# Transposing q and k by DMA from the ninth pair on, with both kinds of scores in one PE visit

## The chip, the cores and the metric

One core of one Trainium2 chip. The time is the device time of a whole execution in microseconds. Ratios are computed as the mean time of one kernel's fast runs over that of the other's fast runs in the same rounds, so they are not quite the ratio of the medians quoted beside them. An interval is the 95% interval of that ratio. "Slow" marks a run more than 1.5% above the fastest of the same kernel; such runs are left out of ratios.

## The reference, cut to what matters

Two attentions over 8 x 8 heads of 576 tokens and 64 dimensions are added, and the sum goes through an MLP.

```python
def _attn_ref(q, k, v):
    # q_d, k_d, v_d: means of groups of 4 tokens (144 groups)
    out_d = sm_attn(q_d, k_d, v_d)              # full attention over the groups
    out_up = np.repeat(out_d, 4, axis=2)
    mask = np.abs(pos[:, None] - pos[None, :]) < 4
    scores = np.where(mask, 0.125 * q @ k.T, -1e9)  # local attention, a band of 7
    ...
    return out_up + softmax(scores) @ v

def _moe_ref(x, w_in, w_out):                   # 4608 x 512 -> 2048 -> 512
    h = x @ w_in
    return (h / (1 + np.exp(-h))) @ w_out
```

## The kernel before

Heads go in 32 pairs. The Python program has a planner: it simulates the engines with a guessed cost for each instruction, takes whatever it believes ready, and so fixes at build time the order of instructions on each engine and on each DMA queue. On the chip every engine and queue works strictly in that order, waiting on semaphores. Pairs 0 to 7 ("direct") use another form of the softmax sums and of the v means; the change leaves them alone.

For a pair from the ninth on, the parts that matter:

```python
def load_qk(p):      # SP queue: qs, ks, 96 partitions x (2 heads x 6 tokens x 64), float32
def cast(p):         # POOL: qs -> qb, ks -> kb, bf16
def ph_T(p):         # PE: 6 + 6 transposes of 96 x 128 into PSUM
    ...
        P.op("PE", lambda t: t.transpose(tps[:, 96*c:96*c+96], w, id_bf[:, :]), ...)
    # out of PSUM, tokens put in their order on the way
    P.op("DVE", lambda e: e.tensor_copy(dst[0], src[0]), ...)          # qT
    P.op("ACT", lambda e: e.activation(dst[1], src[1], AF.Copy), ...)  # kT
def do_mean(p, nm):  # DVE: sums of 4 tokens, qT -> qd, kT -> kd
def ph_S1(p):        # PE: 8 local scores (row mode), ACT: exp
def ph_S2(p):        # PE: 2 local + 4 group scores, ACT: exp
def ph_Z(z):         # PE: softmax sums of two pairs; ACT: zc
    for o in range(4):                       # four copies of one partition to ten
        P.op("SP", dma_start(zr[10*o:10*o+10, :], zsrc[32*o:32*o+1, :] ...), ...)
def do_recip(z):     # DVE: rr = 1/zr; SP: scr (device memory) <- rr
def do_bcast(z):     # SP: four broadcasts Rb <- scr
def ph_PV(p):        # PE: attention x v;  DVE: xo = that x Rb;  POOL: xT += xo
```

"Row mode" is a setting of PE in which a matmul uses 64 of its 128 rows. The attention works through two PSUM buffers called duo. The MLP's first matmul (hps) reads xT; its second (ops) gives the output. In the planner every DMA of the SP queue is charged 450 units of issue and lands 2200 units after its bytes:

```python
t += 450 if eng == "SP" else 650 if eng == "ACT" else 800
...
q[0][0].end = t + 2200
```

The softmax here doesn't subtract the row's maximum and nothing guards it: scores larger than these inputs give would overflow.

## Time and profile before

| | before |
|---|---|
| median (range) of the 3 runs known at the prediction | 410.2 us (408.15 to 411.78) |
| span of the profiled run, granted clock (share of full speed that PE was given) | 410.4 us, 0.978 |
| PE busy over the span | 363.9 us (89%) |
| SP queue issuing in the stage of pairs 8 to 31 | 78% |

The lines that carry the reading are in the prediction. One row more, since the pace of the stage is read from it: the groups of q summed on DVE, once in each pair from 8 to 31 (minimum/median/maximum ns, first and last start in us).

```profile
L407 DVE TENSOR_REDUCE qd<-qT x24: 685/744/754, 86.2 to 284.8; 128x144 bf16<-128x576 bf16 x24
```

From 86.2 to 284.8 us there are 23 periods of 8.63 us. "SP issuing" is worked out from the timeline of the SP queue: the union of its issue intervals between these two starts, over their distance. The timeline shows successive issues of one line as one row with the gaps between them; without these gaps the figures of this kind are 0.1 to 0.4 us per pair lower. Issuing of a DMA doesn't count as busy in the profile's own tables, so such a queue has no row of its own in the page.

### The profile page before, as it was taken

Reading aid. Unit: us, or ns where it says so; the run is one execution under the profiler, and the core shown is the slowest. Engines: PE = TensorE matmul, PEld = TensorE weight load, DVE = VectorE, ACT = ScalarE, POOL = GpSimd, SP = SyncE. Lnnn points to the kernel's source line nnn. Section 1 sums busy time; section 2 is a strip of 40 time slices with the busy share of each in tenths; the row PEclk is TensorE's granted clock in tenths of the full one; section 3 lists DMA queues with packets and bytes.
Section 4 is the critical chain, followed back from the end, with each engine's and each line's share of the span. In section 5 each row is a group of like instructions: output and inputs, shape, how many; then the busy total and the mean of one; then the engine's idle time right before and its main releaser. Section 6 shows DMA issues by size and latency. Waiting matters only on the chain.

```text
span 410.4 us, 7839 instructions
## 1 busy us (share of the span) xinstructions
PE 363.9 (89%) x3145; PEld 232.8 (57%) x3184; DVE 229.5 (56%) x341; ACT 218.6 (53%) x378; POOL 181.8 (44%) x257
## 2 busy tenths in 40 slices
PE   1445889998899999979999798989999999999996
PEld 1225868676556556645656455655565555565552
DVE  1340342885667668787788877787645343343320
ACT  3361155854785567655776556757543444344331
POOL 7998456843943286376274627644404000000000
PEclk9999886999999999998999999999999999999999
DMA  6489743899899859886989954996232000101012
GB/s 172 98 194 316 196 91 89 177 212 204 190 214 245 238 134 235 172 220 176 245 225 207 194 184 136 253 187 168 98 102 88 26 26 33 46 27 51 26 53 77
DMA packets 77628, 61.81 MB, mean 151 GB/s; under 512 B 46616, under 2 KB 67864, under 8 KB 77592
## 3 DMA queue, kind: packets, MB, share of 16 engines
q1 hardware_dynamic: 73368, 55.02, 55.5%
q0 software_dynamic: 4224, 6.29, 6.9%
q8 instruction: 25, 0.41, 0.5%
q14 instruction: 11, 0.09, 0.1%
HBM read 53.67 MB, written 9.58 MB: 154 GB/s over the span
## 4 chain that ended last, share of the span: by engine, by line
PE 71%; POOL 8%; DMA 8%; ACT 4%; DVE 4%; issue 3%; SPq 1%; POOLq 0%; ACTq 0%
PE hps L378 29%; PE ops L378 28%; PE duo L378 11%; DMA vs<-in_v_dram 6%; PE duo L388 3%; DVE Pt L443 2%; DMA zr<-zc 2%; POOL hs L402 2%; ACT vb L354 1%; ACT th L640 1%; POOL qb L349 1%; POOL xo L512 1%; POOL kb L349 1%; POOL w_in_sb L668 1%; ACT Rb L577 1%
## 5 line engine op out<-in xcount | busy, mean ns | idle before, releaser
L378 PE MATMUL hps<-xT,w_in_sb 128*128 128x512 f32 x576 | 175.6, 431 | 0.8 <-DVE gT L642 0.7
L642 DVE SCALAR_TENSOR_TENSOR gT<-th,hps 128x512 bf16<-128x512 f32 x144 | 98.7, 687 | 108.0 <-ACT th L640 107.2
L378 PE MATMUL ops<-w_out_bf,gT 128*128 128x512 bf16 x537 | 139.0, 383 | 4.2 <-issue 2.9
L640 ACT ACTIVATE th<-hps 128x512 f32<-128x512 f32 x144 | 86.0, 597 | 94.4 <-PE hps L378 94.1
L378 PEld LDWEIGHTS hps<-xT,w_in_sb 128*128 128x128 f32 x576 | 106.0, 189 | 32.2 <-DVE gT L642 2.5
L378 PEld LDWEIGHTS ops<-w_out_bf,gT 128*128 128x128 bf16 x576 | 46.4, 98 | 65.0 <-issue 23.1
L617 POOL TENSOR_TENSOR xT<-xo 128x576 fp32r<-128x576 f32 (+2 forms) x40 | 40.7, 1031 | 92.7 <-DVE xo L600 92.4
L443 DVE TENSOR_TENSOR Pt<-Pt,mask_bf 128x1152 bf16<-128x1152 bf16 x32 | 38.0, 1188 | 19.5 <-ACT Pt L435 19.3
L349 POOL CAST qb<-qs 96x768 bf16<-96x768 f32 x31 | 27.1, 874 | 20.3 <-DMA qs<-in_q_dram 14.3
L359 POOL TENSOR_TENSOR vt<-vq 72x512 f32<-72x512 f32 x24 | 32.3, 1347 | 8.2 <-DMA vq<-in_v_dram 7.5
L661 ACT ACTIVATE osb<-ops 128x512 f32<-128x512 f32 x36 | 21.6, 599 | 21.6 <-PE ops L378 21.4
L420 ACT ACTIVATE Pt<-duo 128x912 bf16<-128x912 f32 x32 | 29.7, 927 | 3.6 <-PE duo L378 3.5
L354 ACT ACTIVATE vb<-vs 128x640 bf16<-128x640 f32 x32 | 23.4, 732 | 14.3 <-DMA vs<-in_v_dram 9.8
L598 DVE TENSOR_TENSOR xo<-duo,Rb 128x456 f32<-128x456 f32 x32 | 20.0, 624 | 19.4 <-PE duo L378 18.6
L393 DVE COPY qT<-duo 128x576 bf16<-128x576 bf16 x32 | 23.9, 750 | 10.7 <-PE duo L388 10.4
L349 POOL CAST kb<-ks 96x768 bf16<-96x768 f32 x31 | 25.7, 829 | 3.2 <-DMA ks<-in_k_dram 3.2
L378 PE MATMUL duo<-gT 128*128 128x90 f32 x128 | 23.5, 361 | 3.7 <-POOL gT L516 3.2
L378 PEld LDWEIGHTS duo<-gT 128*128 128x128 f32 x128 | 22.9, 274 | 4.4 <-POOL gT L516 3.5
L378 PE MATMUL duo<-qT,kT 64*128 64x112 bf16 (+1 forms) x320 | 20.4, 226 | 4.0 <-DVE xo L598 1.3
L394 ACT ACTIVATE kT<-duo 128x576 bf16<-128x576 bf16 x32 | 20.8, 649 | 4.2 <-PE duo L388 4.0
L388 PE MATMUL duo<-id_bf,qb 96*128 96x96 bf16 x192 | 14.6, 216 | 7.4 <-POOL xo L303 4.7
L378 PEld LDWEIGHTS duo<-qT,kT 64*128 64x128 bf16 x320 | 11.0, 99 | 17.6 <-issue 6.5
(65 smaller groups left out, 301.0 us busy)
## 6 DMA issues: line engine op xcount, KB each, us to landing
vs<-in_v_dram SPq DMA_DIRECT2D x64, 160.0 KB, 4.2
qs<-in_q_dram SPq DMA_DIRECT2D x32, 288.0 KB, 5.1
ks<-in_k_dram SPq DMA_DIRECT2D x32, 288.0 KB, 5.9
out_dram<-osb SPq DMA_DIRECT2D x36, 256.0 KB, 2.1
Rb<-scr SPq DMA_DIRECT2D x48, 180.0 KB, 3.8
vq<-in_v_dram SPq DMA_DIRECT2D x24, 256.0 KB
w_in_sb<-in_moe_w_in_dram POOLq DMA_DIRECT2D x4, 1024.0 KB, 8.1
w_out_bf<-in_moe_w_out_dram POOLq DMA_DIRECT2D x4, 512.0 KB, 14.5
```

What stands on the lines that cost most here:

```text
L349: pool(lambda g, d=dst, s=src: g.tensor_copy(d, s), r=[R(f"{nm}s{i}")], w=[R(f"{nm}b{j}")], cost=830)
L354: P.op("ACT", lambda e: e.activation(vb[m][:, :, :], vs[i][:, :, :], AF.Copy), r=[R(f"vs{i}")], w=[R(f"vb{m}")], cost=730)
L359: pool(lambda g: g.tensor_tensor(vt[:, :, :], vq[i][:, :, 0:128], vq[i][:, :, 128:256], ALU.add), r=[R(f"vq{i}")], w=[R("vt")], cost=1290)
L378: return P.op("PE", lambda t: t.matmul(out_, lhsT, rhs, start=start, stop=stop, skip_group_check=True), r, w, cost=cost)
L388: P.op("PE", lambda t, c=c, w=w, tps=tps: t.transpose(tps[:, 96 * c:96 * c + 96], w, id_bf[:, :]), r=[R("id"), R(f"{nm}b{j}")], w=[bk[x]], ...
L393: P.op("DVE", lambda e: e.tensor_copy(dst[0], src[0]), r=[bk[0]], w=[R(f"qT{j}")], cost=800)
L420: P.op("ACT", lambda e: e.activation(Pt[m][:, :, 0:456], D[:, :, 0:456], AF.Exp, scale=0.125), r=bk, w=[R(f"P{m}")], cost=930)
L443: P.op("DVE", lambda e: e.tensor_tensor(Pt[m][:, :, :], Pt[m][:, :, :], mask_bf[:, :].unsqueeze(1).to_broadcast([128, 2, S_]), ALU.mult), ...
L617: P.op("POOL", lambda e, dst=dst, in0=in0, in1=in1: e.tensor_tensor(dst, in0, in1, ALU.add), r=[R(f"xo{x}")], w=xblk(kc, t, e_), cost=200 ...
L640: P.op("ACT", lambda e: e.activation(th[tb][:, :], hps[hb][:, :], AF.Tanh, scale=0.5), r=[R(f"h{hb}", True)], w=[R(f"th{tb}")], cost=600)
L642: P.op("DVE", lambda e: e.scalar_tensor_tensor(gT[j % 2][:, f, :], th[tb][:, :], 1.0, hps[hb][:, :], ALU.add, ALU.mult), r=[R(f"h{hb}", Tr ...
L661: P.op("ACT", lambda e: e.activation(osb[s_][:, :], ops[ob][:, :], AF.Copy, scale=0.5), r=[R(f"o{ob}", True)], w=[R(f"osb{s_}")], cost=600)
```

## The change

Its intent is to take the transposes off PE, the fullest engine. The casts qb and kb are transposed between SBUF buffers by DMA; DVE and ACT then put the tokens in order from SBUF instead of from PSUM; and since both kinds of scores can now be formed at once, they share one visit of PE in row mode. The core of the diff:

```diff
+        qr = sb("qr", [128, 6, 96], BF16, 2)
+        kr = sb("kr", [128, 6, 96], BF16, 2)
...
+        def load_T(p, x):
+            j = p % 2
+            src, dst = (qb, qr) if x == "q" else (kb, kr)
+            P.op("SP", lambda e: e.dma_start_transpose(
+                dst[j][:, :, :], src[j][:, :, :, :].rearrange("p c h d -> p (c h d)")),
+                r=[R(f"{x}b{j}")], w=[R(f"{x}r{j}")], dma=f"{x}r{j}", cost=700)
+            P.free["SP"] += 700
+
+        def order_T(p, x):
+            j, y = p % 2, p % NQT
+            src = (qr if x == "q" else kr)[j][:, :, :].rearrange("p r g -> p g r")
+            dst = (qT if x == "q" else kT)[y][:, :].rearrange("p (g r) -> p g r", r=6)
+            if x == "q":
+                P.op("DVE", lambda e: e.tensor_copy(dst, src), ...)
+            else:
+                P.op("ACT", lambda e: e.activation(dst, src, AF.Copy), ...)
...
-            task(attn, f"T{p}", "PE", [f"c{p}", nm("S2", p - 2)], ...)
-            task(attn, f"S1{p}", "PE", [f"T{p}", nm("PV", p - NP_)], ...)
-            task(attn, f"S2{p}", "PE", [f"S1{p}", f"mq{p}", f"mk{p}"], ...)
+            if p in direct:
+                ...                                  # as before
+            else:
+                task(attn, f"S2{p}", "PE", [tq, tk, f"mq{p}", f"mk{p}", nm("PV", p - NP_)], ...,
+                     lambda: [R(f"duo{d}{x}", True) for d in range(2) for x in "ab"],
+                     lambda p=p: (ph_S1(p), ph_S2(p)), "row")
```

More of the change, by code (lines that the diff above doesn't have):

```diff
@@ L249, in bass_hourglass_attn__then__act_silu_kernel @@
         vd = sb("vd", [72, 4, 64], BF16, NVB)
-        qT = sb("qT", [128, S_], BF16, 2)
-        kT = sb("kT", [128, S_], BF16, 2)
+        NQT = 2
+        qT = sb("qT", [128, S_], BF16, NQT)
+        kT = sb("kT", [128, S_], BF16, NQT)
+        qr = sb("qr", [128, 6, 96], BF16, 2)
+        kr = sb("kr", [128, 6, 96], BF16, 2)
         hs = sb("hs", [128, 288], F32)
@@ L318, in load_qk @@
                     w=[R(f"{nm}{i}")], dma=f"{nm}{i}", cost=1050)
+        def load_T(p, x):
[10 more added lines that the diff above has]
+            if x == "q":
+                P.op("DVE", lambda e: e.tensor_copy(dst, src), r=[R(f"qr{j}")], w=[R(f"qT{y}")], cost=700)
+            else:
+                P.op("ACT", lambda e: e.activation(dst, src, AF.Copy), r=[R(f"kr{j}")], w=[R(f"kT{y}")], cost=700)
         def load_v(p):
@@ L391, in ph_T @@
             src = [D[:, x, 0:288].bitcast(BF16).rearrange("p (r g) -> p g r", r=6) for x in range(2)]
-            dst = [t[j][:, :].rearrange("p (g r) -> p g r", r=6) for t in (qT, kT)]
-            P.op("DVE", lambda e: e.tensor_copy(dst[0], src[0]), r=[bk[0]], w=[R(f"qT{j}")], cost=800)
-            P.op("ACT", lambda e: e.activation(dst[1], src[1], AF.Copy), r=[bk[1]], w=[R(f"kT{j}")], cost=700)
+            y = p % NQT
+            dst = [t[y][:, :].rearrange("p (g r) -> p g r", r=6) for t in (qT, kT)]
+            P.op("DVE", lambda e: e.tensor_copy(dst[0], src[0]), r=[bk[0]], w=[R(f"qT{y}")], cost=800)
+            P.op("ACT", lambda e: e.activation(dst[1], src[1], AF.Copy), r=[bk[1]], w=[R(f"kT{y}")], cost=700)
         def do_mean(p, nm):
-            j = p % 2
+            j, y = p % 2, p % NQT
             src, dst = (qT, qd) if nm == "q" else (kT, kd)
             if p in direct:
-                s2 = src[j][:, :].rearrange("p (g r) -> p g r", r=2)
+                s2 = src[y][:, :].rearrange("p (g r) -> p g r", r=2)
                 h2 = hs[:, :].rearrange("p (g r) -> p g r", r=2)
                 pool(lambda e: e.tensor_tensor(hs[:, :], s2[:, :, 0], s2[:, :, 1], ALU.add),
-                     r=[R(f"{nm}T{j}")], w=[R("hs")], cost=820)
+                     r=[R(f"{nm}T{y}")], w=[R("hs")], cost=820)
                 pool(lambda e: e.tensor_tensor(dst[j][:, :], h2[:, :, 0], h2[:, :, 1], ALU.add),
@@ L407, in do_mean @@
             P.op("DVE", lambda e: e.tensor_reduce(
-                dst[j][:, :], src[j][:, :].rearrange("p (g r) -> p g r", r=4), mybir.AxisListType.X, ALU.add),
-                r=[R(f"{nm}T{j}")], w=[R(f"{nm}d{j}")], cost=680)
+                dst[j][:, :], src[y][:, :].rearrange("p (g r) -> p g r", r=4), mybir.AxisListType.X, ALU.add),
+                r=[R(f"{nm}T{y}")], w=[R(f"{nm}d{j}")], cost=680)
         def ph_S1(p):
             D, bk = next_duo()
-            j, m = p % 2, p % NP_
+            j, m, y = p % 2, p % NP_, p % NQT
             for c in range(4):
@@ L416, in ph_S1 @@
                     rows = slice(64 * h, 64 * h + 64)
-                    mm(D[:, h, QB[c]:QB[c] + NQ[c]], kT[j][rows, W0[c]:W0[c] + 128],
-                       qT[j][rows, QB[c]:QB[c] + NQ[c]], [R(f"kT{j}"), R(f"qT{j}")], [bk[h]],
+                    mm(D[:, h, QB[c]:QB[c] + NQ[c]], kT[y][rows, W0[c]:W0[c] + 128],
+                       qT[y][rows, QB[c]:QB[c] + NQ[c]], [R(f"kT{y}"), R(f"qT{y}")], [bk[h]],
                        cost=26, m="row")
@@ L424, in ph_S2 @@
             D, bk = next_duo()
-            j, m = p % 2, p % NP_
+            j, m, y = p % 2, p % NP_, p % NQT
             for h in range(2):
                 rows = slice(64 * h, 64 * h + 64)
-                mm(D[:, h, 0:120], kT[j][rows, 448:576], qT[j][rows, 456:576],
-                   [R(f"kT{j}"), R(f"qT{j}")], [bk[h]], cost=30, m="row")
+                mm(D[:, h, 0:120], kT[y][rows, 448:576], qT[y][rows, 456:576],
+                   [R(f"kT{y}"), R(f"qT{y}")], [bk[h]], cost=30, m="row")
             for s in range(2):
@@ L713, in bass_hourglass_attn__then__act_silu_kernel @@
             z = p // 2
+            y = p % NQT
+            tq, tk = (f"T{p}", f"T{p}") if p in direct else (f"oq{p}", f"ok{p}")
+            if p not in direct:
+                for x in "qk":
+                    task(side, f"t{x}{p}", "SP", [f"c{p}", nm(f"o{x}", p - 2)], [R(f"{x}b{j}")],
+                         [R(f"{x}r{j}")], lambda p=p, x=x: load_T(p, x))
+                    task(side, f"o{x}{p}", "DVE" if x == "q" else "ACT",
+                         [f"t{x}{p}", nm("S2", p - NQT), nm(f"m{x}", p - NQT)], [R(f"{x}r{j}")],
+                         [R(f"{x}T{y}")], lambda p=p, x=x: order_T(p, x))
             task(side, f"lqk{p}", "SP", [nm("c", p - NST), before.get(f"lqk{p}")], [],
@@ L719, in bass_hourglass_attn__then__act_silu_kernel @@
                  lambda p=p: castw(p))
-            task(side, f"c{p}", "POOL" if p >= NEARLY else "DVE", [f"lqk{p}", nm("T", p - 2)],
+            task(side, f"c{p}", "POOL" if p >= NEARLY else "DVE", [f"lqk{p}"] + ([nm("T", p - 2)] if p - 2 in direct or p < 2 else [nm("tq", p - 2), nm("tk", p - 2)]),
                  [R(f"qs{i}"), R(f"ks{i}")], [R(f"qb{j}"), R(f"kb{j}")], lambda p=p: cast(p))
             if p in direct:
-                done.add(f"cv{p}")
+                done.update((f"cv{p}", f"oq{p}", f"ok{p}"))
             else:
@@ L727, in bass_hourglass_attn__then__act_silu_kernel @@
             for x in "qk":
-                task(side, f"m{x}{p}", "POOL" if p in direct else "DVE", [f"T{p}"], [R(f"{x}T{j}")], [R(f"{x}d{j}")],
+                task(side, f"m{x}{p}", "POOL" if p in direct else "DVE", [tq if x == "q" else tk, nm("S2", p - 2)], [R(f"{x}T{y}")], [R(f"{x}d{j}")],
                      lambda p=p, x=x: do_mean(p, x))
@@ L736, in bass_hourglass_attn__then__act_silu_kernel @@
                      [R(f"scr{z % 2}")], [R(f"Rb{(p - 1) % NR}"), R(f"Rb{u}")], lambda z=z: do_bcast(z))
-            task(attn, f"T{p}", "PE", [f"c{p}", nm("S2", p - 2)], [R(f"qb{j}"), R(f"kb{j}")], duo_w,
-                 lambda p=p: ph_T(p))
-            task(attn, f"S1{p}", "PE", [f"T{p}", nm("PV", p - NP_)], [R(f"qT{j}"), R(f"kT{j}")], duo_w,
-                 lambda p=p: ph_S1(p), "row")
-            task(attn, f"S2{p}", "PE", [f"S1{p}", f"mq{p}", f"mk{p}"], [R(f"qd{j}"), R(f"kd{j}")], duo_w,
-                 lambda p=p: ph_S2(p), "row")
+            if p in direct:
+                task(attn, f"T{p}", "PE", [f"c{p}", nm("S2", p - NQT), nm("mq", p - NQT), nm("mk", p - NQT)],
+                     [R(f"qb{j}"), R(f"kb{j}")], duo_w, lambda p=p: ph_T(p))
+                task(attn, f"S1{p}", "PE", [f"T{p}", nm("PV", p - NP_)], [R(f"qT{y}"), R(f"kT{y}")], duo_w,
+                     lambda p=p: ph_S1(p), "row")
+                task(attn, f"S2{p}", "PE", [f"S1{p}", f"mq{p}", f"mk{p}"], [R(f"qd{j}"), R(f"kd{j}")], duo_w,
+                     lambda p=p: ph_S2(p), "row")
+            else:
+                task(attn, f"S2{p}", "PE", [tq, tk, f"mq{p}", f"mk{p}", nm("PV", p - NP_)],
+                     [R(f"qT{y}"), R(f"kT{y}"), R(f"qd{j}"), R(f"kd{j}")],
+                     lambda: [R(f"duo{d}{x}", True) for d in range(2) for x in "ab"],
+                     lambda p=p: (ph_S1(p), ph_S2(p)), "row")
             if p in direct:
```

## The prediction

> **What bounds the kernel now.** I read the table of stretches first, because a share of the whole span mixes three stages. Columns: stretch in us, its length, busy us of PE, PEld, DVE, ACT and POOL with instruction counts, granted clock, DMA share, GB/s.
>
> ```profile
> 100.00:310.00 210.00, 197.27 (x1743) 120.78 (x1770) 155.35 (x230) 135.59 (x231) 110.81 (x120) 0.99 0.80 190
> 310.00:411.00 101.00, 96.23 (x445) 54.92 (x450) 34.23 (x51) 37.05 (x62) 3.32 (x3) 0.99 0.11 42
> 0.00:100.00 100.00, 70.38 (x961) 57.12 (x965) 39.97 (x60) 45.98 (x85) 67.70 (x136) 0.93 0.78 176
> ```
>
> The reader is to see that the middle 210 us, where the changed pairs 8 to 31 run beside the MLP, has PE busy for 197.27 us (94%) and DVE for 74%; no compute engine but PE is near full. The last 100 us are MLP alone, work that was left over. So work taken off PE in the middle is filled with MLP and shortens the tail, as long as the order of instructions fits. That order is fixed when the program is built: a late operand stalls PE even if MLP work is waiting behind it.
>
> Second, the chain that ended last, in order of time, for a quiet piece of that stage (start, us, what):
>
> ```profile
> 211.31 0.93 PE hps L378 x4
> 212.24 0.88 PE ops L378 x4
> 213.12 0.28 PE duo L378 x6
> 213.41 0.62 PE duo L388 x12
> 214.02 0.99 PE hps L378 x4
> ...
> 215.89 0.28 PE duo L378 x6
> 216.18 1.14 PE hps L378 x4
> 217.32 0.53 PE duo L388 x12
> 217.85 0.86 PE ops L378 x4
> ```
>
> The chain is PE, back to back. The visit of twelve transposes (L388) is 0.53 to 0.62 us of it, the visit of six scores 0.28 us, and the four hps matmuls after a visit that ends in scores take 1.14 us instead of 0.93.
>
> Third, because the added work goes to the SP queue, that queue's own issues (minimum/median/maximum ns) and its longest waits, the waits in the middle stage only:
>
> ```profile
> L316 SPq DMA_DIRECT2D qs<-in_q_dram x32: 312/440/1619, 0.8 to 261.3; - x32
> L316 SPq DMA_DIRECT2D ks<-in_k_dram x32: 313/449/1559, 1.3 to 261.7; - x32
> L327 SPq DMA_DIRECT2D vs<-in_v_dram x64: 368/522/2762, 16.5 to 281.4; - x64
> L332 SPq DMA_DIRECT2D vq<-in_v_dram x24: 607/686/6439, 75.6 to 281.9; - x24
> L334 SPq DMA_DIRECT2D vq<-in_v_dram x24: 494/504/1441, 76.4 to 282.7; - x24
> L471 SPq DMA_DIRECT2D zr<-zc x48: 697/722/865, 112.4 to 300.1; - x48
> L488 SPq DMA_DIRECT2D Rb<-scr x48: 451/596/1388, 134.0 to 306.6; - x48
> ```
> ```profile
> SPq L663 <- ACT osb L661: 17.5, 10, 3.3
> SPq L479 <- DVE rr L477: 12.2, 6, 2.8
> SPq L488 <- DMA scr<-rr: 11.2, 6, 3.1
> ```
>
> Per pair this is 0.44 + 0.45 for q and k, 2 x 0.52 for v, 0.69 + 0.50 for the grouped v, half of (4 x 0.72 + 0.32 + 4 x 0.60) = 2.80 for the softmax sums (the 0.32 is the median issue of scr), and 0.33 for 0.9 output stores of 0.364: 6.25 us. The pair period is 8.63 us (the first and last reduction of qT on DVE start at 86.2 and 284.8 us, 23 periods apart). So SP issues for 72% of the time, and waits in line for most of the rest. It has slack only where those waits can shrink: the waits for output tiles (17.5 us) are waits for PE itself.
>
> **What the Trainium skill says.** "VectorE: DVE Perf Modes", section "The three transpose paths", gives a 128x128 bf16 transpose 390 ns on TensorE and 1309 ns by the DMA crossbar. Here six 96x128 transposes that follow one another take about 0.3 us of PE, so pipelined ones are far cheaper than 390 ns each; no run so far shows the crossbar. "DMA: Bandwidth & Descriptors", section "Latency and other measured facts", gives the DMA transpose 261 GB/s where the middle dimension is not contiguous; no trace yet. The same page, section "DMA Transpose (X-bar)", speaks of a crossbar tile of 16 partitions by 128 columns: one of our 96x768 sources is 6 x 6 = 36 tiles. "TensorEngine Tiling (Array Packing)", section "Key Properties", says that a change of tiling mode drains TensorE; the 1.14 against 0.93 us above agrees (0.21 us).
>
> **The change, part by part.** Removed from PE: for 24 pairs, a visit of 12 transposes. 24 x 0.57 us (middle of 0.53 and 0.62) = 13.7 us, all on the chain. Scores of both kinds in one visit save one return from row mode per pair, at most 24 x 0.21 = 5.0 us; where the transposes followed the scores directly they had taken most of that drain, so I count 3 us. Together 16.7 us of PE, if nothing else moves.
>
> Moved: the copies of q and k out of PSUM (DVE 0.75 us, ACT 0.65 us) become reorders from SBUF with the same 576 columns. The strided source gives no reason for a large gain; at most a tenth of a us each, on engines that do not bound. One PSUM slot per pair is freed, but the score visit now wants both slots free at once.
>
> Added: 48 crossbar transposes. Data: 96 x 768 x 2 = 147,456 bytes each; at 261 GB/s an estimate of 0.56 us with all DMA engines, so 48 x 0.56 = 27 us of DMA time over 24 x 8.63 = 207 us, or 0.13 on a share of 0.80. SP issue: no trace shows it. If each of 36 tiles is handed out separately it costs more than a plain copy; I take 1.0 to 1.3 us, an estimate by analogy with the small but scattered zr copies (0.72 us) against the large q loads (0.44). The kernel's own planner charges the queue 450 + 700 = 1150 units of ns, a choice of its writer and not a measurement. With 1.15: 2 x 1.15 = 2.3 us per pair, 8.55 us of issue per pair against a period of 8.63. Add the unavoidable wait for the scr copy (11.2 us over 24 pairs, 0.47) and SP wants about 9.0 us per pair. So the attention stage should stretch by 24 x 0.4 = about 10 us.
>
> Stretching costs nothing in itself: the MLP left over at the end (about 97 us) can fill it, if the planner puts it there. Its charges (q, k, v, sums and stores 7.0 us per pair, times 1.1, now plus 2 x 0.7 x 1.1) make it plan about 9.2 us of DMA per pair instead of 7.7, which is close to what I expect of SP. So the interleaving should roughly fit.
>
> Latency is added too: cast, then issue and landing of a transpose (about 1.2 + 4 us, the landing taken from the 4.2 to 5.9 us of loads), then reorder, where it was 0.6 + 0.75. With two buffers at each step a transpose may run about one pair ahead, 8.6 us, so this is hidden when SP is not late.
>
> Sum: 410.2 - 16.7 + about 6 us of new stalls of PE from late operands (half of the stretch, by judgement) = about 400 us.
>
> **Rivals.** (1) SP becomes the bound. For it: the queue is already always issuing or waiting, and it works in order, so a transpose that waits for a cast holds up the loads behind it. If a transpose issues in 2 us or more, SP wants 6.25 + 4 + 0.5 = 10.8 us per pair, 2.2 above the period, 50 us in all, of which the planned order covers perhaps half: 410 - 17 + 25 = about 418, up to 440. Against it: 17.5 us of the waits are for PE and shrink when PE is early. (2) DMA becomes the bound: share 0.80 + 0.13 = 0.93 on average, with stretches now at 1.0; loads then land later than 5 to 6 us and casts follow late. I take this at 5 to 10 us, about 402 to 408; it would look like same. (3) All is hidden and the freed PSUM slot also removes some of the 13 us in which PE is idle in the middle stage: 388 to 392.
>
> **Range and chances.** The main line is 400; full success is 388, a costly issue 418 to 440. I give rival 1 a little over 0.2, rival 2 a quarter, and the rest to the main line and rival 3. The 8-in-10 range is 385 to 426. Faster by over 2% means below 402.0, slower means above 418.4: chances 0.49, 0.29 and 0.22.
>
> **What would show it.** Right: no group of 12 transposes after about 90 us; a visit of 14 scores of about 0.5 us with one slow hps after it; the tail of pure MLP shorter by 10 us or more, not longer; PE still 93% busy or more in the middle. The median issue of a transpose on SP tests the 1.15 us directly, its landing time the 4 us, the DMA share of the middle the 0.93. Wrong: PE waiting for ACT or DVE writers of kT, qT, kd in sums above 20 us, or the SP queue without a wait for output tiles while POOL casts and vb wait longer for loads (rival 1 or 2: the issue time says which).

## The result, and the profile after

The changed kernel takes 432.93 us (429.33 to 435.8, 4 runs, the slowest of them a slow one) against 409.38 us (408.15 to 411.78, 4 runs): a ratio of 1.0538, interval 1.0432 to 1.0644. It is slower by 5.4%, outside the predicted range of 385 to 426 us.

The stretches of the changed kernel, with the columns explained in the prediction:

```profile
100.00:310.00 210.00, 176.32 (x1250) 100.44 (x1272) 132.07 (x196) 126.04 (x204) 101.71 (x107) 0.94 0.94 202
310.00:430.00 120.00, 114.00 (x649) 67.03 (x659) 54.73 (x86) 52.97 (x88) 15.86 (x14) 1.00 0.27 73
```

In the middle 210 us PE is busy for 176.32 us where it was busy for 197.27 us, and its granted clock is 0.94 instead of 0.99. The rest has grown from 101 to 120 us. The sums over the whole span close: PE is busy for 360.9 us instead of 363.9 us (3.0 less), and idle for 429.4 - 360.9 = 68.5 us instead of 410.4 - 363.9 = 46.5 us (22.0 more); 22.0 - 3.0 = 19.0 us is the difference of the spans. So the removed work did not come back as time: PE stood idle instead.

The added work in rows (the SP queue's issue of each transpose, the two reorders, and the pace of the stage):

```profile
L326 SPq DMA_TRANSPOSE qr<-qb x24: 1196/1274/3440, 85.5 to 316.4; - x24
L326 SPq DMA_TRANSPOSE kr<-kb x24: 1206/1272/2477, 89.0 to 317.8; - x24
L336 DVE COPY qT<-qr x24: 548/710/1587, 96.3 to 323.3; 128x576 bf16<-128x576 bf16 x24
L338 ACT ACTIVATE kT<-kr x24: 1167/1192/1257, 97.0 to 322.8; 128x576 bf16<-128x576 bf16 x24
L428 DVE TENSOR_REDUCE qd<-qT x24: 734/753/754, 97.1 to 326.3; 128x144 bf16<-128x576 bf16 x24
```

Each transpose holds the queue for 1.27 us. From issue to landing they take 4.2 us (q) and 3.3 us (k) in the median, no more than the loads of q and k do (4.3 and 4.8 us). The period is now (326.3 - 97.1) / 23 = 9.97 us, and SP issues for 9.03 us of it: 91%. On the queue's list of waits no entry above 4.8 us is left in the stage: the wait for output tiles, 14.5 us between 86 and 286 us before, is 4.8 us between 96 and 324 us after. New are 16 us of waits, in all, ahead of the transposes, for casts and other work of POOL. The loads of q and k do not land later than before (medians 4.3 and 4.8 us, before 5.1 and 5.9), and yet the casts of q wait 37.3 us for them over the span where they waited 14.3: the loads are issued late.

```profile
POOL qb L349 <- DMA qs<-in_q_dram: 14.3, 6, 5.3
POOL qb L369 <- DMA qs<-in_q_dram: 37.3, 15, 10.3
```

These are POOL's waits (in total, times, the longest), first before and then after.

The clearest single piece is a stall of PE near 155 us. First, PE's timeline with the idle time ahead of a group and what ended it; then the chain that ended last for the same piece (start, us, what):

```profile
152.00 0.73 PE L398 MATMUL hps<-xT,w_in_sb 128*128 128x512 f32 x2
160.07 0.79 PE L398 MATMUL hps<-xT,w_in_sb 128*128 128x512 f32 x1 [7.35 <-POOL xT L638]
```
```profile
146.42 0.37 SPq L500
...
148.07 0.72 SPq L352
148.84 0.51 SPq L354
...
149.39 0.34 SPq L319
149.76 0.45 SPq L319
...
150.25 0.78 SPq L492
...
153.84 0.53 SPq L509
...
154.41 3.67 DMA Rb<-scr
...
159.15 1.35 POOL xT L638 x2
```

PE waits 7.35 us for xT. POOL could form xT only when DVE had multiplied by the factors Rb, and these arrived at 158.08 us, 3.67 us after the end of the issue of their broadcast, which began at 153.84 us. The value that they broadcast had been sent to device memory at 146.42 us. In between SP does not rest: it issues v loads (L347, in the lines left out), grouped v, q and k loads for later pairs (L352, L354, L319), the four sums of the next two pairs (L492) and an output store, one behind another. Here the chain of the kernel runs through the issue of DMAs, which it hardly did before: SP's sequencer has 12% of the chain after, and had 1% before.

This is one form of the stalls. On PE's list of waits between 96 and 326 us, 8.0 us are waits of hps for xT, and 16.1 us are waits of hps and ops for DVE's gT, which stands behind ACT's th (before, between 86 and 286 us, the waits for gT were 0.2 us). The largest of these, in ACT's and PE's timelines:

```profile
228.42 1.17 ACT L338 ACTIVATE kT<-kr 128x576 bf16<-128x576 bf16 x1 [4.33 <-DMA kr<-kb]
230.35 1.17 ACT L338 ACTIVATE kT<-kr 128x576 bf16<-128x576 bf16 x1 [0.77 <-DMA kr<-kb]
232.78 1.65 PE L398 MATMUL hps<-xT,w_in_sb 128*128 128x512 f32 x3 [4.99 <-DVE gT L663]
```

ACT, in its fixed order, waits for a transposed k and does the th of the MLP only afterwards, and PE waits for that. The first k in question had been cast by 213.3 us; its transpose was issued at 223.98 us, behind v loads, another transpose, broadcasts and sums on the queue.

And the idle time is paid twice. The stretches around the stall (the figure behind the five busy times with their counts is the granted clock, the next the DMA share):

```profile
155.00:160.00 5.00, 0.00 (x0) 0.00 (x0) 2.02 (x4) 0.00 (x0) 2.04 (x4) 0.73 0.82 237
160.00:165.00 5.00, 3.77 (x19) 2.13 (x20) 3.65 (x6) 3.28 (x5) 4.24 (x7) 0.50 0.89 191
```

When PE resumes at 160 us its clock is at 0.50. By the trace's clock records it fell at 157.3 us, 4.5 us after PE had stopped, and rose again at 167.5 us. "TensorE: Matmul & The Clock Gate", section "Part 1: The HAM clock gate", says that the clock of PE is halved after an idle window of about 3.4 us and released by a busy one. This agrees with it: the clock falls in the stall, and the first hps matmul after it takes 0.79 us, where one that follows a wait at 225.00 us, at the full clock, takes 0.50 us.

### The profile page after: what moved, and what is told of

It reads as the page before. It is cut to its first block, busy times and chain, and to the rows that moved or that the text cites. A ratio compares the mean times of both kernels' runs of the same rounds, so it can differ in the third digit from the quotient of the medians.

```text
span 429.4 us, 7337 instructions
## 1 busy us (share of the span) xinstructions
PE 360.9 (84%) x2861; PEld 223.5 (52%) x2896; DVE 226.4 (53%) x341; ACT 227.2 (53%) x378; POOL 186.6 (43%) x257
## 3 DMA queue, kind: packets, MB, share of 16 engines
q1 hardware_dynamic: 102552, 62.10, 65.2%
## 4 chain that ended last, share of the span: by engine, by line
PE 41%; POOL 13%; DMA 12%; SPq 12%; DVE 8%; ACT 7%; issue 6%; POOLq 0%; ACTq 0%; DVEq 0%
PE hps L398 18%; PE ops L398 16%; PE duo L398 6%; DMA vq<-in_v_dram 4%; DMA Rb<-scr 3%; DMA qr<-qb 3%; DVE gT L663 2%; SPq L492 2%; ACT th L661 2%; SPq L347 2%; SPq L326 2%; POOL vt L379 2%; SPq L352 2%; POOL xT L638 1%; DMA kr<-kb 1%
## 5 line engine op out<-in xcount | busy, mean ns | idle before, releaser
L398 PE MATMUL hps<-xT,w_in_sb 128*128 128x512 f32 x576 | 173.4, 434 | 21.7 <-DVE gT L663 13.6
L398 PEld LDWEIGHTS hps<-xT,w_in_sb 128*128 128x128 f32 x576 | 108.0, 194 | 59.3 <-DVE gT L663 22.0
L398 PEld LDWEIGHTS ops<-w_out_bf,gT 128*128 128x128 bf16 x576 | 48.6, 99 | 72.9 <-issue 20.3
L369 POOL CAST qb<-qs 96x768 bf16<-96x768 f32 x31 | 28.7, 926 | 43.2 <-DMA qs<-in_q_dram 37.3
L338 ACT ACTIVATE kT<-kr 128x576 bf16<-128x576 bf16 x24 | 28.7, 1200 | 24.1 <-DMA kr<-kb 24.1
L464 DVE TENSOR_TENSOR Pt<-Pt,mask_bf 128x1152 bf16<-128x1152 bf16 x32 | 31.4, 980 | 17.1 <-ACT Pt L456 17.1
L374 ACT ACTIVATE vb<-vs 128x640 bf16<-128x640 f32 x32 | 23.4, 735 | 16.3 <-DMA vs<-in_v_dram 14.8
L336 DVE COPY qT<-qr 128x576 bf16<-128x576 bf16 x24 | 20.9, 871 | 4.3 <-DMA qr<-qb 4.1
L398 PE MATMUL duo<-qT,kT 64*128 64x112 bf16 (+1 forms) x320 | 17.9, 228 | 6.0 <-ACT kT L338 2.6
L381 POOL TENSOR_TENSOR vd<-vt 72x256 bf16<-72x256 f32 x24 | 21.7, 903 | 1.9
L458 ACT ACTIVATE Pd<-duo 72x576 bf16<-72x576 f32 x32 | 20.7, 646 | 0.0
```

Of the source, the lines that this page charges most:

```text
L338: P.op("ACT", lambda e: e.activation(dst, src, AF.Copy), r=[R(f"kr{j}")], w=[R(f"kT{y}")], cost=700)
L369: pool(lambda g, d=dst, s=src: g.tensor_copy(d, s), r=[R(f"{nm}s{i}")], w=[R(f"{nm}b{j}")], cost=830)
L374: P.op("ACT", lambda e: e.activation(vb[m][:, :, :], vs[i][:, :, :], AF.Copy), r=[R(f"vs{i}")], w=[R(f"vb{m}")], cost=730)
L381: pool(lambda g: g.tensor_tensor(vd[m][:, :, :], vt[:, :, 0:64], vt[:, :, 64:128], ALU.add), r=[R("vt")], w=[R(f"vd{m}")], cost=750)
L398: return P.op("PE", lambda t: t.matmul(out_, lhsT, rhs, start=start, stop=stop, skip_group_check=True), r, w, cost=cost)
L464: P.op("DVE", lambda e: e.tensor_tensor(Pt[m][:, :, :], Pt[m][:, :, :], mask_bf[:, :].unsqueeze(1).to_broadcast([128, 2, S_]), ALU.mult), ...
```

## The experiments

The theories at the start. **A:** SP's issue time; 48 transposes of 1.27 us go into a queue that was issuing for 78% of the stage. **B:** the capacity of the DMA engines (share 0.94 in the middle). **C:** the build-time plan, which does not know how long issues and landings take. **D:** the joint score visit, or the slower reorder. All kernels give a correct result unless said otherwise. The columns are as defined above; the stage is that of pairs 8 to 31, PE busy and DMA share are those of 100 to 310 us. The profiled runs of e14, e15 and e17 were slow ones, so their last four columns are only a hint. The DMA share adds up packet times, so it can pass 1. Unless it is said that the order was compared, the planner made a new order for a kernel, and that alone can move the time: e16 is a new order for before and takes 1.6% longer.

| run | median us | ratio to before (interval) | SP issue per pair, share | period us | PE busy us | DMA share |
|---|---|---|---|---|---|---|
| before | 409.4 | 1 | 6.76, 78% | 8.63 | 197.3 | 0.80 |
| after | 432.9 | 1.054 (1.043 to 1.064) | 9.03, 91% | 9.97 | 176.3 | 0.94 |
| e1 joint visit, PE transposes | 412.5 | 1.007 (1.000 to 1.014) | 6.77, 70% | 9.66 | 201.1 | 0.76 |
| e2 DMA transposes, two visits | 437.4 | 1.067 (1.059 to 1.074) | 9.31, 92% | 10.13 | 182.5 | 0.97 |
| e3 before + idle transposes | 447.5 | 1.092 (1.084 to 1.100) | 9.34, 91% | 10.26 | 180.2 | 0.92 |
| e4 before + tiny copies | 451.5 | 1.099 (1.089 to 1.109) | 9.27, 90% | 10.28 | 175.1 | 0.67 |
| e5 after, planner's issue times | 433.9 | 1.061 (1.053 to 1.069) | 9.09, 91% | 9.97 | 181.2 | 1.00 |
| e6 transposes from ACT | 441.3 | 1.077 (1.069 to 1.086) | 6.96, 68% | 10.21 | 171.3 | 1.07 |
| e7 after, cheaper fold | 423.6 | 1.036 (1.028 to 1.045) | 8.12, 86% | 9.47 | 183.4 | 1.03 |
| e8 after, sums from ACT | 465.4 | 1.136 (1.127 to 1.145) | 6.57, 60% | 10.87 | 167.4 | 0.95 |
| e9 after, q and k loads from POOL | 435.4 | 1.061 (1.049 to 1.072) | 8.34, 84% | 9.94 | 177.7 | 0.95 |
| e10 after, e9 + grouped v from POOL + fold | 448.2 | 1.097 (1.089 to 1.105) | 6.50, 64% | 10.21 | 167.3 | 0.94 |
| e11 before, cheaper fold | 416.5 | 1.019 (1.012 to 1.026) | 5.80, 60% | 9.70 | 197.0 | 0.77 |
| e12 e1 + cheaper fold | 410.5 | 1.005 (0.994 to 1.015) | 5.71, 61% | 9.42 | 199.1 | 0.77 |
| e13 after, thin v loads (wrong result) | 424.0 | 1.032 (1.026 to 1.038) | 8.44, 88% | 9.57 | 183.8 | 0.77 |
| e14 e10 + thin v loads (wrong result) | 438.6 | 1.067 (1.059 to 1.074) | 5.61, 56% | 9.95 | 171.6 | 0.82 |
| e15 after, planner's issues and landings | 436.0 | 1.058 (1.050 to 1.066) | 9.08, 93% | 9.74 | 178.6 | 0.96 |
| e16 before, the same planner | 416.4 | 1.016 (1.010 to 1.023) | 6.72, 70% | 9.61 | 197.3 | 0.78 |
| e17 after, lightened (wrong result) | 417.0 | three of four runs slow, see text | 6.20, 69% | 9.03 | 186.1 | 0.64 |
| e18 before, lightened (wrong result) | 407.1 | 0.989 (0.979 to 0.998) | 4.05, 48% | 8.46 | 201.4 | 0.45 |

### The two halves of the change (e1, e2)

e1 puts the transposes back on PE and keeps the joint visit:

```diff
             else:
+                task(attn, f"T{p}", "PE", [f"c{p}", nm("S2", p - NQT), ...],
+                     [R(f"qb{j}"), R(f"kb{j}")], duo_w, lambda p=p: ph_T(p))
                 task(attn, f"S2{p}", "PE", [tq, tk, f"mq{p}", f"mk{p}", ...], ...)
```

> The changed kernel with the transposes of pairs 8 to 31 back on PE, and the scores of both kinds still in one visit. Theory A (the SP queue: 48 transposes of 1.27 us issue fill a queue that was already 79% issuing) and theory B (the DMA engines are full: share 0.94) both expect the loss to vanish: 400 to 412 us. Theory D (the joint score visit that wants both PSUM slots, or the plan's new task order, does the harm) expects 422 us or more.

e2 keeps the DMA transposes and splits the visit:

```diff
-                task(attn, f"S2{p}", "PE", [tq, tk, f"mq{p}", f"mk{p}", ...], ...,
-                     lambda p=p: (ph_S1(p), ph_S2(p)), "row")
+                task(attn, f"S1{p}", "PE", [tq, tk, nm("PV", p - NP_)], ..., lambda p=p: ph_S1(p), "row")
+                task(attn, f"S2{p}", "PE", [f"S1{p}", f"mq{p}", f"mk{p}"], ..., lambda p=p: ph_S2(p), "row")
```

> The changed kernel with the transposes by DMA but the two kinds of scores in two PE visits as before. A and B expect the loss to stay: 425 to 442 us. D expects it to go: 415 us or less.

e1 took 412.48 us (0.5 us above the range that A and B gave), e2 437.36 us. The whole loss comes with the transposes by DMA, and D as the joint visit falls. The joint visit alone gains nothing that these runs resolve. The middle of e1:

```profile
100.00:310.00 210.00, 201.11 (x1708) 120.49 (x1708) 144.65 (x221) 130.69 (x225) 107.30 (x116) 0.98 0.76 181
```

e1 is instructive in another way: its period is 9.66 us, a good 1 us above that of before, and yet PE is busy for 201.11 of 210 us and the time is that of before. A longer stage costs nothing as long as PE is kept at work in it.

### The queue or the bytes (e3, e4)

Both take the kernel before, with PE, DVE, ACT and POOL given the very same instructions in the same order (compared instruction by instruction), and add work to the SP queue alone, behind each cast from pair 8 on. The planner's clock is set back, so that it does not know of them. Nobody reads the results.

```diff
+            if p not in direct:
+                for u, (nm, st) in enumerate((("q", qb), ("k", kb))):
+                    # e3: one transpose
+                    P.op("SP", lambda e: e.dma_start_transpose(qr[2*u+j], st[j] ...), r=[R(f"{nm}b{j}")], ...)
+                    # e4 instead: two copies of one partition to ten, 1.4 KB each
+                    P.op("SP", lambda e: e.dma_start(dz[4*v_+2*u+j], st[j][0:1, ...][:, 0:720] ...), ...)
```

> The kernel before, every compute engine's order unchanged, with 48 DMA transposes of the cast q and k into buffers that nobody reads, put into the SP queue where the casts are planned. A expects SP issuing over 90% of the middle stage and 425 to 445 us; B expects about the same (the bytes and the small packets are there too); a theory that blames the reorder copies (ACT 1.19 us instead of 0.65) or the PE order expects 405 to 415.

> The same as e3_before_dummyT, but each transpose is replaced by two tiny copies of one partition to ten (1.4 KB each) of some 0.7 us issue each: about the same SP time, a hundredth of the bytes. A expects nearly the time of e3_before_dummyT (within 2% of it, 425 us or more). B expects 408 to 415 us, the time of before.

They took 447.52 us (2.5 us above the range of A) and 451.51 us. The issues of e4, and its middle:

```profile
L356 SPq DMA_DIRECT2D dz<-qb x48: 697/733/869, 88.2 to 317.5; - x48
L356 SPq DMA_DIRECT2D dz<-kb x48: 697/697/1460, 89.9 to 318.9; - x48
```
```profile
100.00:310.00 210.00, 175.12 (x1466) 103.74 (x1466) 123.50 (x186) 112.92 (x192) 98.72 (x108) 0.93 0.67 169
```

Four tiny copies per pair hold the queue for 2 x 0.733 + 2 x 0.697 = 2.86 us, a little more than two transposes (2.54 us). The DMA share falls to 0.67, below that of before, and PE still loses as much as it does in the changed kernel: busy 175.12 us at a clock of 0.93. The copies wait for little (about 7 us in all in the stage, by the queue's list of waits), so it is not that they hold up the queue by waiting for a cast; nor does a cast wait for them, by POOL's list. A is shown to be sufficient: issue time on the queue, with next to no bytes, gives the loss. B is not needed for it. Both kernels lose more than the changed one (9.2 and 9.9% against 5.4%). They have the queue's new load without the relief of PE, and 447.5 - 432.9 = 14.6 us is near the 13.7 us that the prediction gave the transposes; but the two orders differ, so that this is the value of the relief is not shown.

### The planner (e5, e15, e16)

```diff
-            t += 450 if eng == "SP" else 650 if eng == "ACT" else 800
+            t += ISSUE[...] if eng == "SP" else ...   # qs, ks 450, vs 550, vq 620, zr 740, scr 360, Rb 620, os 440, qr, kr 1300
-            P.free["SP"] += 700
-                P.op("ACT", ... kT ..., cost=700)
+                P.op("ACT", ... kT ..., cost=1190)
 # e15 and e16 also:
-                    q[0][0].end = t + 2200
+                    q[0][0].end = t + 5000
```

> The changed kernel, same instructions, but its build-time planner charges SP the measured issue times (transpose 1300 ns, sums 740 and 360, broadcasts 620, v 550 and 620, stores 440, q and k 450 instead of 450 for all and 1150 for a transpose) and ACT 1190 for the reorder of k. If the loss is a plan that does not know of the queue, so that PE stands in line behind late scores (theory A1), PE is filled again: 395 to 412 us, although the stage of scores stays as long or longer. If the queue's rate alone costs the time, whatever the order (theory A2), 422 us or more.

> The changed kernel with the planner charging the measured issue times (as in e5_after_plan) and a landing 5.0 us after the bytes instead of 2.2 us. Theory C (PE stands in line behind scores planned too early): the stalls of PE go and the MLP fills them, 395 to 415 us. A and B as limits of rate: 425 us or more.

> The kernel before with the same two corrections of its planner. If the plan of before was good enough, 403 to 414 us; a gain of over 2% would mean that the planner, not the transposes, was the thing to change.

Told of the issue times the planner gives 433.89 us; told of the landings too, 436.03 us (one of the four runs slow and left out of the ratio); and the kernel before takes 416.35 us (1.016, above the 403 to 414 us expected; at 2% the verdict is "unclear"). C, in this form, falls: a plan with better averages does not recover the loss. That no order would is not shown.

### Taking time off the queue (e7, e11, e12)

The four copies that fold the sums into 40 partitions, 0.70 us each, become two DMAs by way of device memory:

```diff
-            for o in range(4):
-                P.op("SP", dma_start(zr[i][10*o:10*o+10, :], zsrc[32*o:32*o+1, :] ...), ...)
+            P.op("SP", dma_start(zd[i], zsrc[0:128:32, :]), ...)          # 4 x 720 in device memory
+            P.op("SP", dma_start(zr[i][:, :], zd[i] as 40 x 72), ...)     # as a task of its own
```

> The changed kernel with the four one-partition copies of 0.70 us that fold the softmax sums replaced by two copies by way of device memory (about 0.4 us each): SP has 1.0 us per pair less to issue, the chain of the sums has one landing more (about 2 us). A expects a part of the loss back: 414 to 426 us. B expects no change or worse, 428 us or more.

> The kernel before with the same cheaper fold of the sums as e7_after_zdram: SP from 79% issuing to some 67%. Control: if SP's queue bounds only the changed kernel, this gains little, 402 to 412 us, and less than the 9 us that the changed kernel gained; if it gains as much, the fold is a change of its own.

> PE transposes, the joint score visit, and the cheaper fold: a candidate for better than both. SP is at some 63%. A expects 398 to 412 us; a loss against e1_merge_only would mean that the longer chain of the sums costs more than the queue time it saves.

The same edit makes the changed kernel faster (423.63 us, 1.036 where it was 1.054; the intervals overlap by 0.002), as A expected, and the kernel before takes 416.51 us (1.019; "unclear" at 2%), where A expected 402 to 412 us: a miss. A reading that fits A: in the kernel before the chain of the sums has one landing more and the queue had time to spare; in the changed kernel the 0.9 us of queue time per pair is worth more than the landing. But both kernels have new orders, and 1.8 points down and 1.9 up are of the size that a new order made in e16, so the pair supports A without showing it. e12, the candidate for better than both, is the same as before within 2%.

### Other queues (e6, e8, e9, e10)

```diff
 # e6
-            P.op("SP", lambda e: e.dma_start_transpose(
+            P.op("ACT", lambda e: e.dma_start_transpose(
 # e8
         def chain(z):
-            return "SP"
+            return "ACT"
 # e9: q and k loads of pairs 10 to 31
-                P.op("SP", lambda s: s.dma_start(t[i] ...
+                P.op("POOL", lambda s: s.dma_start(t[i] ...
 # e10: e9, the grouped v loads from POOL as well, and the fold of e7
```

> The changed kernel with the 48 transposes issued from ACT's queue, the planner charging ACT in place of SP. The bytes and the DMA engines are the same. Theory A (SP's queue): SP falls to about 75% issuing and most of the loss goes, 402 to 418 us, if ACT bears 2.5 us more per pair (it was at 60%). Theory B (DMA capacity): 425 us or more.

> The changed kernel with the nine small DMAs per two pairs of the softmax sums issued from ACT (2.8 us per pair off SP, about 3 us per pair onto ACT, which reaches some 90%). A expects 402 to 420 us, with ACT as the next bound; B expects 425 us or more.

> The changed kernel with the q and k loads of pairs 10 to 31 issued from POOL's queue, where the buffer they fill is freed by POOL's own cast, so that they wait for nothing there. SP has 0.89 us per pair less, the DMA engines have the same bytes. A expects part of the loss back: 410 to 424 us. B (DMA capacity) expects 428 us or more.

> The changed kernel with q, k and the grouped v loads issued from POOL and the fold of the sums by way of device memory: SP has 3.1 us per pair less, which is more than the 2.5 us of the transposes, POOL has four issues of some 0.77 us more. A expects the loss gone and, if PE's relief then counts, 392 to 412 us. B expects 425 us or more; a new bound on POOL (48% busy before) would show in casts that come late.

All four missed what A expected. SP falls to 60 to 84% issuing, and the kernels take 441.27, 465.37, 435.39 and 448.16 us. So a freer SP queue is not enough by itself. That the issues, and the waits that go with them, cost time where they land on an engine that computes is a reading; for e6 the trace shows one way: on ACT a transpose is issued in order between activations, and in this piece of ACT's timeline

```profile
210.37 0.60 ACT L682 ACTIVATE osb<-ops 128x512 f32<-128x512 f32 x1 [1.26 <-PE ops L398]
216.63 1.31 ACTq L326 DMA_TRANSPOSE qr<-qb  x1
218.04 1.36 ACT L374 ACTIVATE vb<-vs 128x640 bf16<-128x640 f32 x2 [7.08 <-issue]
```

ACT does nothing for 7.08 us around the issue of one transpose that stands at the head of its order. In e10 the SP queue waits for 32.2 us for DVE's reciprocals, 25.1 us for output tiles and 23.4 us for POOL's casts of q and k (its list of waits between 100 and 330 us), and PE in turn waits for DVE. Which of these links holds e9 and e10 was not isolated; I leave it open.

### The bytes in the changed kernel itself (e13, e14)

The two v loads of each pair from 8 on bring one window of five; the orders and the number of issues stay (compared), the result is wrong on purpose.

```diff
+                n = 5 if p in direct else 1
-                              ap=[[64, 128], [112 * 64, 5], [1, 64]])
+                              ap=[[64, 128], [112 * 64, n], [1, 64]])
```

> The changed kernel, same order on every engine and the same number of issues, but the two v loads of pairs 8 to 31 bring one of their five windows (a fifth of their descriptors; the result is wrong on purpose). The DMA share should fall by about a quarter. If SP's queue holds this kernel (A), the time falls by under 8 us: 425 us or more, apart from what a shorter issue gives. If the DMA engines do (B), 412 us or less.

> The same thin v loads in e10_after_lean, where SP issued only 64% of the time (wrong on purpose too). B expects a large gain there: 448 to 420 us or less. If the planned order or POOL holds it (C), it stays above 435 us.

e13 took 423.98 us, between the two expectations. The DMA share is at 0.77, below that of before, and three fifths of the loss are still there (3.2 of 5.4%). The issue of a v load fell with its size, from a median of 0.526 to 0.438 us, which is 0.6 us of queue time per pair by the table, so a part of the gain is A's. How the 2.2 points divide between bytes and issue is open; as the share is below that of before, B can be at most these two fifths of the loss. In e14 the same cut gained about 3 points on e10 (one run slow) and left it at 1.067: bytes do not hold that kernel either.

### The queue back at its old load (e17, e18)

The fold of e7, the thin loads of e13, and no grouped v loads from pair 10 on, in both kernels:

```diff
-            if p in direct:
+            if p in direct or p >= 10:
                 return
             src = v[b, h:h + 2]...        # the two grouped v loads
```

> The changed kernel with thin v loads (e13), the cheaper fold (e7) and no grouped v loads from pair 10 on (wrong on purpose): SP issues about 6.3 us per pair, what the kernel before has. A (SP's issue time): the loss goes, 395 to 412 us, SP at some 75%. The chain of the pair (the transfer's landing, the reorder of 1.19 us on ACT, buffers of two): it stays, 418 us or more.

> The kernel before with the same three cuts (wrong on purpose). It had room on SP, so A expects little: 404 to 416 us. Its distance to e17_after_light says what the transposes are worth, or cost, when the queue is free.

With SP at 6.20 us per pair, less than before has, the changed kernel ran in 417.53, 417.11, 409.5 and 416.84 us. By the 1.5% rule three of these are slow, at clocks of 0.963 to 0.966 against 0.983, and no ratio is given. Taken as they are, they lie between the same and 2% slower than before's 410.88 us; most of the loss is gone. The median lies between what A and the chain expected. The bytes fell too (DMA share 0.64), so this run does not part A from B. But the lightened kernel before took 407.11 us. So even with the queue at its old load, nothing shows that the transposes by DMA gain over those on PE: the one fast run is 0.8% above the mean of the four of e18 (409.5 over 406.15). (The 4.05 us of queue time for e18 are 3.63 without the gaps between rows.) The middle of the two, e17 first and then e18; the trace of e17 is of a slow run, so the comparison is a hint and no more:

```profile
100.00:310.00 210.00, 186.10 (x1396) 109.79 (x1420) 155.84 (x222) 141.52 (x226) 108.12 (x113) 0.94 0.64 158
```
```profile
100.00:310.00 210.00, 201.42 (x1757) 122.60 (x1784) 153.48 (x232) 136.75 (x233) 112.14 (x120) 0.98 0.45 133
```

In these two PE is idle for 24 us of the middle in e17 and for 8.6 us in e18. If a remainder is real, the longer chain of each pair (one more transfer, a slower reorder) is a candidate; that was not taken apart and stays open.

## Why the prediction was wrong, point by point

- **PE bounds, and work taken off it is filled with MLP: right as a mechanism, and it did not come to pay.** PE was busy with transposes for 24.4 us before and 7.6 us after; for 10.8 of these 16.8 us it did nothing else at the same time. Its busy time fell by only 3.0 us. A part is the clock: PE was busy at the halved clock for 16.9 us before and 28.8 us after, and by an estimate half of the difference, 5.9 us, is time which that added. About 2 us stay unexplained.
- **The issue of a transpose, 1.15 us: nearly right.** It is 1.27 us. **The landing, 4 us: right**, 4.2 and 3.3 us. **The DMA share, 0.93: right by luck**, 0.94. By the packet times of the hardware queue (55.5% of 410.4 us before, 65.2% of 429.4 us after) the transposes took about 52 us of all engines, under the load of the rest, and not the 27 us estimated from 261 GB/s; the longer period thinned the rest by about as much. The loads did not land late, so **rival 2** did not come true in its own terms.
- **SP's time per pair, 9.0 us with the wait: short in its base.** I added medians and had 6.25 us; the mean of before, issues that are held up included, is 6.76 us. After, SP issues for 9.03 us where I had 8.55.
- **The period: the stretch was mis-sized.** Predicted 0.4 us per pair, 10 us in all; measured 9.97 - 8.63 = 1.34 us per pair, 24 x 1.34 = 32 us. A queue with 9.03 us of issue does not run with 9.03 us of period, because it stands still for waits in between (9% of the stage, 11% without the gaps). I added one wait, 0.47 us for the scr copy; that one shrank to 3.5 us in all, and the 16 us ahead of the transposes, 0.7 us per pair, were not in my sum.
- **"So the interleaving should roughly fit": the step that failed.** I allowed 6 us of stalls, "half of the stretch" by judgement (half of 10 would be 5). PE's idle time rose by 22.0 us. That a stretched stage costs nothing in itself was right (e1: 9.66 us and no loss), but there SP has 30% of its time free. At 91% every delay on the in-order queue is passed on, to loads and to the chain of sums alike, and the fixed orders of ACT and PE meet them as waits (the pieces at 155 and 232 us). That the planner's charges were too low was not the reason by itself: with the measured ones the time stayed (e5, e15).
- **The reorder, "at most a tenth of a us": right for q (0.71 after 0.75), wrong for k.** ACT takes 1.19 us from SBUF after 0.65 us from PSUM. ACT does not bound, and how much of the end this costs was not measured.
- **The joint visit, 3 us of gain: not seen** (e1 at 1.007).
- **Rival 1 was the one that came true, and I gave it a little over 0.2.** Its text asked for an issue of 2 us or more; 1.27 us was enough. The sign named for it came in part: the wait for output tiles went from 14.5 to 4.8 us and the casts of q waited 37.3 us, where it had been 14.3; the casts of v on ACT waited no longer (8.5 us, 8.4 before), and the direct waits of PE for kT, qT and kd stayed under 5 us, not 20. Rival 3 did not come. The warning was there before: the view of the queue showed a resource that was always issuing or waiting, and I counted on its waits to shrink.

## What to carry to other kernels

A queue that issues in order is an engine: add up its issue times per unit of work, with the mean and not the median, before giving it more. Work that moves from an engine at 94% to a queue at 78% is no relief if it lands there at 91%, because what waits behind it, in line, is what feeds the first engine. And idle time of PE is charged twice where the clock falls with it.

## What the Trainium skill lacked or had wrong

- "DMA: Bandwidth & Descriptors", section "Issuing engines are not separate DMA queues", calls the sequencer's time to initiate a DMA "usually small relative to the DMA itself". Here a transpose holds SP for 1.27 us of the 3.3 to 4.2 us from issue to landing, a copy of one partition to ten for 0.70 us, and 2.86 us per pair of such copies with hardly any bytes cost 9.9% of the time (e4). For issue times by kind the page has only cycle counts of "previous generations", in its part on trn3, and none for these shapes.
- The same section expects only issue time to be saved by another queue. From ACT it was lost: 1.077 of the time of before, against 1.054 from SP (e6); in one piece ACT did nothing for 7.08 us around the issue of a transpose.
- "VectorE: DVE Perf Modes", section "The three transpose paths", compares 390 ns on TensorE with 1309 ns by the crossbar. No run here has a 128x128 one alone; what mattered is neither, but 0.6 us of PE for twelve pipelined ones against 2.54 us of the issuing queue for two.
- "SBUF — State Buffer" says under "SBUF cachelines" that for bf16 a stride beyond 8 elements pays a penalty, and gives no figure by engine. Here the same reorder with a stride of 96 elements costs ACT 1.19 us for 576 columns (0.65 us from PSUM), and DVE 0.71 us (0.75 us from PSUM). No run varied the stride, so that it is the reason on ACT is not shown.
